# Attention and two dense layers on one core: conversions spread over the opening's turns, sinks copied between exponentials, one addition on GpSimd

## The chip, the cores and the metric

The kernel runs on one core of one Trainium2 chip. The metric is the device time of one execution in microseconds (us); of several executions the median counts. The core has TensorE (PE, matmuls and transposes into PSUM banks), VectorE (DVE), ScalarE (ACT), GpSimd (POOL) and SyncE (SP, which here issues almost all of the loads). Each engine works through its own list in order, and waits on semaphores where it needs another engine's result.

## The reference

```
scores = scale * q @ k^T                      # 2 batches, 8 heads, 768 positions, 64 wide
keep   = is_sink | in_window                  # 4 sinks, a window of 128
scores = where(keep, scores, -1e9); a = exp(scores - max)
a      = a / (sum(a) + 1e-9)
x      = (a @ v), tokens by 512
h = x @ w_in;  x = (max(h, 0) + alpha * min(h, 0)) @ w_out      # 512 -> 2048 -> 512
h = x @ w_in2; out = (h - tanh(h)) @ w_out2                     # 512 -> 2048 -> 512
```

Weights arrive as 64-bit floats and are converted on the chip to 32-bit ones.

## The kernel before

Attention is done in 48 pairs of heads. Pair n belongs to block u = n // 4 of 128 positions, and holds 2 heads. One pair goes through these helpers:

- `s_mm`: the scores by three products of split operands (L272), into two of the four banks "o".
- `s_max` (L281, VectorE): mask and row maximum, one instruction for each of the two heads. It is the first VectorE instruction of a turn.
- `s_exp` (L290, ScalarE): the exponential and its sum.
- `norm_sum`: part 0 adds 1e-9 to the two sums (L296), part 1 takes the reciprocal (L298). `norm` scales (L305), and `sink_copy` (L311) gathers the sink columns after every second pair from block 2 on.
- `t_mm` (L322) transposes the probabilities into bank t or h, `t_ev` (L329, ScalarE) copies them out. `sink_mm` (L344) transposes the sinks into a bank that scores of a later pair use too, and `sink_ev` (L348, ScalarE) copies them out.
- `pv` (L361, L362; L365 for sinks): the product with v. After four pairs `x_h` (L372, ScalarE) and `x_l` (L377, VectorE) split the block's result into a high and a low part.

Operands of the scores are split into high and low parts ahead of time: `kq_hi` (L236, ScalarE) and `kq_lo` (L239, VectorE), called by `splits_hi` and `splits_lo`. A converted weight block costs two halves on ScalarE (L73, L75) and two on VectorE (L77, L79), each over 128x1024 elements; `conv_start` issues the first two and every `conv_step` the next one. `split_w` (L217, ScalarE) and `split_lo` (L222, VectorE) split the converted weights for the products.

The order on each engine is the order in which the program is written (a manual schedule). The opening is a loop of 19 turns (S_LEAD = 19): turn n issues the scores of pair n + 1, maxima and exponentials of pair n, scaling and transposes of pair n - 1 and the product of pair n - 2, with conversions, splits and filler matmuls (`keep_busy`, L505) between. Then come 96 steps g, one for each of 2 layers, 3 chunks of 512 tokens and 16 blocks of 128 hidden columns. A step multiplies x by a block of w_in (`h_mm`, L394, 12 matmuls), copies the result out of its bank (`evac_first`, L401), applies the nonlinearity and splits it, and two steps later multiplies by w_out (`out_mm`, L446, 12 matmuls). In the first chunk all steps share bank h, so the first matmul of step g + 1 waits for the copy of step g. Pairs 19 to 47 are worked off between the products of steps 0 to 28, one in each.

## Time and profile before

| what | value |
|---|---|
| median of 3 runs (lowest, highest) | 658.94 us (657.57, 661.62) |
| the profiled execution, its span | 659.71 us, 657.9 us |
| busy of the span: PE, DVE, ACT, POOL | 97%, 80%, 72%, 0% |
| mean granted TensorE clock, share of full speed | 0.992 |

The span reaches from the first to the last instruction that the profiler saw; 1.8 us of the execution lie around it. The rows below come from timelines: start, duration, engine, line, operation, output and inputs, count, and in brackets how long the engine had been idle before and which result ended that. An instruction can start before its predecessor has drained, so the distance from one start to the next is often shorter than a duration. Windows give, for a stretch, its length, each engine's busy time with its number of instructions, the granted clock of TensorE, and the DMA engines' share and rate.

### The profile page before, as it was taken

Reading aid. Unit: us, or ns where it says so; the run is one execution under the profiler, and the core shown is the slowest. Engines: PE = TensorE matmul, PEld = TensorE weight load, DVE = VectorE, ACT = ScalarE, POOL = GpSimd, SP = SyncE. Lnnn points to the kernel's source line nnn. Section 1 sums busy time; section 2 is a strip of 40 time slices with the busy share of each in tenths; the row PEclk is TensorE's granted clock in tenths of the full one; section 3 lists DMA queues with packets and bytes.
Section 4 is the critical chain, followed back from the end, with each engine's and each line's share of the span. In section 5 each row is a group of like instructions: output and inputs, shape, how many; then the busy total and the mean of one; then the engine's idle time right before and its main releaser. Section 6 shows DMA issues by size and latency. Waiting matters only on the chain.

```text
span 657.9 us, 9271 instructions
## 1 busy us (share of the span) xinstructions
PE 638.5 (97%) x3246; PEld 503.3 (76%) x3251; DVE 528.0 (80%) x1098; ACT 471.4 (72%) x936; POOL 1.7 (0%) x9
## 2 busy tenths in 40 slices
PE   8888899999999999999999999999999999999996
PEld 3555677777777777777888888888888888888885
DVE  7976898999776665649999979888898888888884
ACT  5976888887666555556877767777777777777772
POOL 1000000000000000000000000000000000000000
PEclk9989799999999999999999999999999999999999
DMA  5643344553100000305355500000010000100001
GB/s 153 193 140 110 126 179 144 197 201 115 49 1 17 1 17 1 123 6 192 128 198 191 188 0 1 1 0 1 0 65 0 1 1 0 65 0 1 0 1 70
DMA packets 27176, 47.36 MB, mean 72 GB/s; under 512 B 3184, under 2 KB 15728, under 8 KB 27120
## 3 DMA queue, kind: packets, MB, share of 16 engines
q1 hardware_dynamic: 26400, 46.29, 20.7%
q10 hardware_dynamic: 720, 0.39, 0.3%
q8 instruction: 27, 0.44, 0.3%
q14 instruction: 29, 0.24, 0.1%
HBM read 43.53 MB, written 3.15 MB: 71 GB/s over the span
## 4 chain that ended last, share of the span: by engine, by line
PE 91%; DVE 3%; ACT 2%; DMA 2%; SPq 1%; issue 1%; DVEq 0%; ACTq 0%
PE ps_o L446 40%; PE ps_h L394 23%; PE ps_s L394 9%; PE ps_t L394 9%; PE ps_s L272 2%; PE ps_t L322 2%; PE ps_v L361 2%; PE ps_v L365 2%; PE ps_v L362 1%; DMA raw_qk<-in_qk_dram 1%; DVE pq L281 1%; SPq L181 1%; DVE pq L305 1%; DMA raw<-in_moe_w_in_dram 0%; DVE kq L239 0%
## 5 line engine op out<-in xcount | busy, mean ns | idle before, releaser
L222 DVE SCALAR_TENSOR_TENSOR wl<-wf,wh 128x512 fp32r<-128x512 f32 x192 | 123.4, 683 | 41.8 <-ACT wh L217 41.8
L217 ACT ACTIVATE wh<-wf 128x512 fp32r<-128x512 f32 x192 | 110.7, 628 | 0.1
L394 PE MATMUL ps_h<-x,wh 128*128 128x512 f32 x296 | 97.4, 409 | 3.1 <-ACT t L401 2.9
L446 PE MATMUL ps_o<-gh,wh 128*128 128x512 f32 x192 | 76.5, 398 | 0.0
L446 PE MATMUL ps_o<-gh,wl 128*128 128x512 f32 x192 | 75.0, 391 | 0.0
L446 PE MATMUL ps_o<-gl,wh 128*128 128x512 f32 x192 | 74.8, 390 | 0.0
L446 PE MATMUL ps_o<-wh,gh 128*128 128x512 f32 x192 | 74.7, 389 | 0.0
L446 PE MATMUL ps_o<-wl,gh 128*128 128x512 f32 x192 | 74.7, 389 | 0.0
L446 PE MATMUL ps_o<-wh,gl 128*128 128x512 f32 x192 | 74.7, 389 | 0.0
L394 PEld LDWEIGHTS ps_h<-x,wh 128*128 128x128 f32 x296 | 52.6, 190 | 14.6 <-ACT t L401 3.5
L290 ACT ACTIVATE pq<-pq,nm 128x288 f32<-128x288 f32 (+1 forms) x96 | 48.5, 509 | 20.5 <-DVE nm L281 20.2
L394 PE MATMUL ps_h<-x,wl 128*128 128x512 f32 x148 | 58.7, 397 | 0.2 <-DVE wl L222 0.2
L329 ACT ACTIVATE pt<-ps_t 128x512 f32<-128x512 f32 (+1 forms) x39 | 22.0, 564 | 47.3 <-PE ps_t L322 47.0
L425 ACT ACTIVATE gh<-g 128x512 fp32r<-128x512 f32 x48 | 30.4, 633 | 29.8 <-DVE g L128 29.8
L77 DVE SCALAR_TENSOR_TENSOR wf<-wf,raw 128x1024 int32<-128x1024 int32 x32 | 39.1, 1221 | 7.9 <-ACT raw L75 7.9
L446 PEld LDWEIGHTS ps_o<-gh,wh 128*128 128x128 f32 x192 | 36.1, 188 | 8.4 <-issue 1.4
L446 PEld LDWEIGHTS ps_o<-gh,wl 128*128 128x128 f32 x192 | 36.0, 188 | 7.8
L446 PEld LDWEIGHTS ps_o<-wh,gh 128*128 128x128 f32 x192 | 36.0, 188 | 7.5
L446 PEld LDWEIGHTS ps_o<-wh,gl 128*128 128x128 f32 x192 | 36.0, 188 | 7.5
L446 PEld LDWEIGHTS ps_o<-wl,gh 128*128 128x128 f32 x192 | 36.0, 188 | 7.5
L446 PEld LDWEIGHTS ps_o<-gl,wh 128*128 128x128 f32 x192 | 36.1, 188 | 7.1
L128 DVE COPY_PREDICATED g<-mask,t 128x512 f32<-128x512 int32 x48 | 36.4, 758 | 4.9
(160 smaller groups left out, 1348.9 us busy)
## 6 DMA issues: line engine op xcount, KB each, us to landing
raw<-in_moe_w_in_dram SPq DMA_DIRECT2D x32, 512.0 KB, 3.3
raw<-in_moe_w_out_dram SPq DMA_DIRECT2D x32, 512.0 KB, 4.3
raw_qk<-in_qk_dram SPq DMA_DIRECT2D x92, 64.0 KB, 3.0
vt<-in_v_dram SPq DMA_DIRECT2D x12, 256.0 KB, 2.9
out_dram<-ob SPq DMA_DIRECT2D x2, 1024.0 KB, 4.3
out_dram<-ob SPq DMA_DIRECT2D x3, 256.0 KB, 3.6
vs<-in_vsink_dram SPq DMA_DIRECT2D x2, 256.0 KB, 3.3
raw_qk<-in_qk_dram ACTq DMA_DIRECT2D x4, 64.0 KB, 2.8
```

Of the source, the lines that this page charges most:

```text
L77: nc.vector.scalar_tensor_tensor(di, di, 3, lw, op0=ALU.logical_shift_left, op1=ALU.bitwise_or)
L128: nc.vector.copy_predicated(g, mask.bitcast(I32), t)
L217: nc.scalar.activation(out=hi, in_=src, func=AF.Copy, scale=W_DOWN)
L222: nc.vector.scalar_tensor_tensor(lo, wf[m, f][:, 512 * part:512 * part + 512], W_DOWN, hi, op0=ALU.mult, op1=ALU.subtract)
L272: nc.tensor.matmul(sps[n, a][:, :w], lhsT=kq[l][h, p, at:at + 128], rhs=kq[r][h, p, K_EVEN:K_EVEN + w], start=e == 0, stop=e == 2)
L290: nc.scalar.activation(out=e, in_=e, func=AF.Exp, scale=-1.0, bias=nm[:, 2 * n + a:2 * n + a + 1], accum_out=sums[G][:, hh:hh + 1])
L322: nc.tensor.transpose(t[:, 256 * a + 128 * e:256 * a + 128 * e + 128], pq[G][:, hh + a, c:c + 128], ident)
L329: nc.scalar.activation(out=ptb[n][:, :, e0:, :], in_=tv[:, :, e0:, :], func=AF.Copy)
L361: nc.tensor.matmul(d, lhsT=vt[u - 1][:, h * D:(h + 1) * D], rhs=pt[:, a, 0, :], start=p == 0, stop=False)
L394: nc.tensor.matmul(h_ps[f], lhsT=w, rhs=x[:, r, kk, :], start=at == 0, stop=at == 11)
L425: nc.scalar.activation(out=gh, in_=mid[f], func=AF.Copy)
L446: nc.tensor.matmul(o, lhsT=l, rhs=r, start=f == 0 and e == 0, stop=f == NF - 1 and e == 2)
```

## The change

In the opening a conversion is issued one part per turn instead of two parts of ScalarE in one turn, and the conversion of block 2 begins there, in turns 16 and 17, instead of in step 0. `splits_hi` runs in the odd turns ahead of the exponentials, in the same turn as its `splits_lo`, and from step 1 on in the same step as it. `sink_ev` stands between the two exponentials instead of before both maxima. The last turn no longer issues the product of pair 16 and three fillers; step 0 starts with the 8 products that need only the high part of x, and the product of pair 16, the scores of pair 19 and the transposes of pair 17 follow. In step 0 the weights of step 1 are split before the maxima of pair 19 instead of after. The addition of 1e-9 is issued on GpSimd. `h_mm` counts single matmuls instead of threes, and `norms` is defined earlier.

```diff
             if part == 0:
-                nc.vector.tensor_scalar(r, r, 1e-9, None, op0=ALU.add)
+                nc.gpsimd.tensor_scalar(r, r, 1e-9, None, op0=ALU.add)
...
-            for G in {0: (0, 2), 1: (1,)}.get(n, (n // 2 + 2,) if n % 2 != (n < S_LEAD - 1) else ()):
+            early = n < S_LEAD
+            for G in {0: (0, 2), 1: (1,)}.get(n, (n // 2 + 1 + early,) if n > 2 and n % 2 == early else ()):
...
-                tps[n - 1] = ps_tile(["t", "h"])
+                tps[n - 1] = ps_tile("th" if n < S_LEAD - 3 else "ht"[n % 2])
                 keep_busy({0: 4, 1: 3, 2: 8}.get(n, 2), tps[n - 1])
             if n >= 2:
                 t_ev(n - 2)
-                if has_sinks(n - 2):
-                    sink_ev(n - 2)
+                if 3 <= n < S_LEAD - 2:
+                    splits_hi(n)
             s_max(n, 0)
             s_max(n, 1)
             s_exp(n, 0)
+            if n >= 2 and has_sinks(n - 2):
+                sink_ev(n - 2)
             s_exp(n, 1)
+            if n == S_LEAD - 2:
+                pv(n - 2)
             if last:
                 x_l(n - 3)
-                pv(n - 2)
-                keep_busy(3, ps_tile(["h"]))
-            if n == S_LEAD - 2:
-                pv(n - 2)
...
             for f, at in CONV0:
                 if n == at:
-                    conv_start(0, f)
-                if at < n < at + 5:
+                    conv_start(0, f, 1)
+                if at < n < at + 4:
                     conv_step(0, f)
...
             if n == S_LEAD - 3:
                 split_lo(0, 0, 0, 0)
+                conv_start(0, 2, 1)
+            if n == S_LEAD - 2:
+                conv_step(0, 2)
...
                     a_loads(n)
-                    h_mm(m, c, f, 0, 3, FIRST)
+                    h_mm(m, c, f, 0, 8, FIRST)
+                    pv(n - 3)
+                    split_w(*steps[1], 0)
+                    norms(n - 1)
+                    split_lo(*steps[1], 0)
+                    splits_lo(n - 2)
+                    s_mm(n)
                     turned(n - 2)
-                    conv_start(0, 2)
-                    h_mm(m, c, f, 3, 4, FIRST)
-                    norms(n - 1)
-                    scores(n)
+                    h_mm(m, c, f, 8, 12, FIRST)
                     conv_step(0, 2)
-                    split_w(*steps[1], 0)
-                    split_lo(*steps[1], 0)
+                    for a in range(2):
+                        s_max(n, a)
+                        s_exp(n, a)
                     evac_first(m, c, f)
                     conv_step(0, 2)
                     load_w(0, 4)
```

On ScalarE, turns 12 and 13 before: copy of transposes, two exponentials, operand split, both halves of a conversion, then turn 13's copy, sinks and exponentials.

```order
L329 ACTIVATE pt<-ps_h 128x512
L290 ACTIVATE pq,sums<-pq,nm 128x288 x2
L236 ACTIVATE kq<-raw_qk 128x2x256
L73 ACTIVATE wf,seen<-raw_90 128x1024
L75 ACTIVATE raw_90<-raw_90 128x1024
L329 ACTIVATE pt<-ps_t 128x512
L348 ACTIVATE pts<-ps_o 128x128
L290 ACTIVATE pq,sums<-pq,nm 128x288 x2
L372 ACTIVATE x<-ps_v 128x4x128
```

The same two turns now:

```order
L329 ACTIVATE pt<-ps_h 128x512
L290 ACTIVATE pq,sums<-pq,nm 128x288 x2
L73 ACTIVATE wf,seen<-raw_90 128x1024
L329 ACTIVATE pt<-ps_t 128x512
L236 ACTIVATE kq<-raw_qk 128x2x256
L290 ACTIVATE pq,sums<-pq,nm 128x288
L348 ACTIVATE pts<-ps_o 128x128
L290 ACTIVATE pq,sums<-pq,nm 128x288
L372 ACTIVATE x<-ps_v 128x4x128
L75 ACTIVATE raw_90<-raw_90 128x1024
```

One half of the conversion and the operand split moved into turn 13, and the sinks between its exponentials.

On VectorE, the maxima and the reciprocal of turn 13 before, with what each waits for:

```order
L281 ISA pq,nm<-ps_o,m_odd 128x288 [waits PE_49]
L281 ISA nm 128x1
L281 ISA pq,nm<-ps_o,m_odd 128x288 [waits Activation_49]
L281 ISA nm 128x1
L296 TENSOR_SCALAR sums<-sums 128x2
L298 RECIPROCAL sums<-sums 128x2 [waits DVE_49]
```

And now:

```order
L281 ISA pq,nm<-ps_o,m_odd 128x288 [waits PE_49]
L281 ISA nm 128x1
L281 ISA pq,nm<-ps_o,m_odd 128x288 [waits PE_49]
L281 ISA nm 128x1
L298 RECIPROCAL sums<-sums 128x2 [waits Pool_49]
```

The second maximum waited for ScalarE (the sink copy) and now waits for TensorE alone; the reciprocal waits for GpSimd.

On TensorE, from the fillers of the last turn to the first products of step 1 before (wh_701 belongs to step 0, wh_892 to step 1; rows of the same kind left out):

```order
L505 MATMUL ps_h<-idle 128x512
L394 MATMUL ps_h<-x,wh_701 128x512
...
L322 MATMUL ps_t<-ident,pq 128x128 x4
L344 MATMUL ps_o<-ident,sk 128x128
L394 MATMUL ps_h<-x,wh_701 128x512 x3
L272 MATMUL ps_o<-kq 128x288 x6
L322 MATMUL ps_t<-ident,pq 128x128 x4
L394 MATMUL ps_h<-x,wh_892 128x512 x2
```

And now (wh_699 and wh_856), from the transposes of pair 16 on:

```order
L322 MATMUL ps_t<-ident,pq 128x128 x4
L394 MATMUL ps_h<-x,wh_699 128x512
...
L361 MATMUL ps_v<-pt,vt 64x128
L362 MATMUL ps_v<-pt,vt 64x128
...
L272 MATMUL ps_o<-kq 128x288 x6
L322 MATMUL ps_t<-ident,pq 128x128 x4
L344 MATMUL ps_o<-ident,sk 128x128
L394 MATMUL ps_h<-x,wh_699 128x512 x4
L322 MATMUL ps_t<-ident,pq 128x128 x4
L394 MATMUL ps_h<-x,wh_856 128x512 x2
```

The product of pair 16 moved behind the first 8 matmuls of step 0, the scores of pair 19 ahead of its last 4, and the fillers are gone.

## Rows read from the trace of the kernel before

**Rows 1.** Windows of 20 us, the end of the opening and the first chunk

```profile
60.00:80.00 20.00, 16.86 (x88) 12.19 (x89) 13.98 (x35) 15.04 (x32) 0.00 (x0) 0.83 0.21 68
80.00:100.00 20.00, 20.00 (x114) 15.55 (x113) 19.72 (x44) 17.16 (x36) 0.00 (x0) 1.00 0.50 183
```

**Rows 2.** Timeline of VectorE, turn 10, to the first maximum of turn 11

```profile
29.99 0.45 DVE L281 CUSTOM_DVE_ANT_0 pq<-ps_o,m_even 128x288 f32<-128x288 f32 x1
...
30.74 0.16 DVE L296 TENSOR_SCALAR sums<-sums 128x2 f32<-128x2 f32 x1
30.94 0.17 DVE L298 RECIPROCAL sums<-sums 128x2 f32<-128x2 f32 x1
31.14 0.65 DVE L305 TENSOR_SCALAR pq<-pq,sums 128x288 f32<-128x288 f32 x2
...
31.97 0.68 DVE L377 TENSOR_TENSOR x<-ps_v,x 128x512 fp32r<-128x512 f32 x1
32.57 1.22 DVE L79 SCALAR_TENSOR_TENSOR wf<-raw,wf 128x1024 int32<-128x1024 int32 x1
33.70 0.45 DVE L281 CUSTOM_DVE_ANT_0 pq<-ps_o,m_even 128x288 f32<-128x288 f32 x1
```

**Rows 3.** Timeline of ScalarE, the end of turn 12 and the start of 13

```profile
37.74 0.63 ACT L236 ACTIVATE kq<-raw_qk 128x512 fp32r<-128x512 f32 x1
38.28 1.15 ACT L73 ACTIVATE wf<-raw 128x1024 f32<-128x1024 f32 x1
...
39.41 1.12 ACT L75 ACTIVATE raw<-raw 128x1024 int32<-128x1024 uint16 x1
40.43 0.57 ACT L329 ACTIVATE pt<-ps_t 128x512 f32<-128x512 f32 x1
40.91 0.26 ACT L348 ACTIVATE pts<-ps_o 128x128 f32<-128x128 f32 x1
```

**Rows 4.** Timeline of VectorE, maxima of pairs 8, 12, 13 (second), 16

```profile
23.98 0.45 DVE L281 CUSTOM_DVE_ANT_0 pq<-ps_o,m_even 128x288 f32<-128x288 f32 x1
...
36.02 0.45 DVE L281 CUSTOM_DVE_ANT_0 pq<-ps_o,m_odd 128x288 f32<-128x288 f32 x1
...
41.20 0.46 DVE L281 CUSTOM_DVE_ANT_0 pq<-ps_o,m_odd 128x288 f32<-128x288 f32 x1 [2.75 <-ACT pts L348]
...
51.41 0.45 DVE L281 CUSTOM_DVE_ANT_0 pq<-ps_o,m_even 128x288 f32<-128x288 f32 x1
```

**Rows 5.** Timeline of TensorE, a turn with sinks, then steps 1 and 2

```profile
36.52 0.71 PE L365 MATMUL ps_v<-pts,vs 128*128 128x128 f32 x4
37.16 0.67 PE L272 MATMUL ps_o<-kq 64*128 64x288 f32 x6
...
38.20 0.60 PE L322 MATMUL ps_t<-ident,pq 128*128 128x128 f32 x4
...
39.43 0.66 PE L272 MATMUL ps_o<-kq 64*128 64x288 f32 x6
...
67.75 1.22 PE L394 MATMUL ps_h<-x,wh 128*128 128x512 f32 x2 [2.89 <-ACT t L401]
...
75.78 0.73 PE L394 MATMUL ps_h<-x,wh 128*128 128x512 f32 x2
```

**Rows 6.** Timeline of GpSimd, a fill and an index pattern at the start

```profile
0.75 0.53 POOL L507 MEMSET idle<- 128x512 bf16 x1 [0.29 <-POOLq L1045]
1.30 0.24 POOL L509 IOTA rel_i<- 128x128 int32 x1
```

**Rows 7.** Timeline of ScalarE, the operand split of turn 8 and x of turn 17

```profile
26.02 0.63 ACT L236 ACTIVATE kq<-raw_qk 128x512 fp32r<-128x512 f32 x1 [0.34 <-DMA raw_qk<-in_qk_dram]
...
57.30 0.60 ACT L372 ACTIVATE x<-ps_v 128x512 fp32r<-128x512 f32 x1 [1.09 <-PE ps_v L365]
```

**Rows 8.** Timelines of VectorE and ScalarE in step 2

```profile
81.96 1.29 DVE L222 SCALAR_TENSOR_TENSOR wl<-wf,wh 128x512 fp32r<-128x512 f32 x2
...
82.40 0.62 ACT L236 ACTIVATE kq<-raw_qk 128x512 fp32r<-128x512 f32 x1
```

More of the change, by code (lines that the diff above doesn't have):

```diff
@@ L390, in h_mm @@
                 h_ps[f] = ps_tile(["hst"[turn[0] % 3]])
-            for at in range(3 * lo, 3 * hi):
+            for at in range(lo, hi):
                 kk, l, r = order[at]
@@ L564, in fast_path, with conv_start @@
         convs = {}
-        def conv_start(m, f):
+        def conv_start(m, f, k=2):
             convs[m, f] = conv_w(m, f)
-            next(convs[m, f])
-            next(convs[m, f])
+            conv_step(m, f, k)
         def conv_step(m, f, k=1):
@@ L573, in conv_step, with norms @@
                 next(convs[m, f], None)
+        def norms(n):
+            norm_sum(n, 0)
+            norm_sum(n, 1)
+            norm(n)
+            sink_copy(n)
         for n in range(S_LEAD):
@@ L590, in fast_path @@
             s_exp(n, 0)
+            if n >= 2 and has_sinks(n - 2):
+                sink_ev(n - 2)
             s_exp(n, 1)
+            if n == S_LEAD - 2:
+                pv(n - 2)
             if last:
                 x_l(n - 3)
-                pv(n - 2)
-                keep_busy(3, ps_tile(["h"]))
-            if n == S_LEAD - 2:
-                pv(n - 2)
             if n >= 1:
-                norm_sum(n - 1, 0)
-                norm_sum(n - 1, 1)
-                norm(n - 1)
-                sink_copy(n - 1)
+                norms(n - 1)
                 if not last:
@@ L608, in fast_path @@
                 pv(n - 2)
-            splits_hi(n)
+            if n < 3:
+                splits_hi(n)
             if n >= 5 and n % 4 == 1:
                 x_h(n - 2)
-            splits_lo(n)
+            if n < S_LEAD - 2:
+                splits_lo(n)
+            if last:
+                splits_hi(n - 1)
             if n >= 5 and n % 4 == 2 and not last:
@@ L622, in fast_path @@
                 if n == at:
-                    conv_start(0, f)
-                if at < n < at + 5:
+                    conv_start(0, f, 1)
+                if at < n < at + 4:
                     conv_step(0, f)
-                if n == at + 3:
+                if n == at + 3 and f + 2 < NF:
                     load_w(0, f + 2)
@@ L678, in turned @@
                 sink_ev(n)
-        def norms(n):
-            norm_sum(n, 0)
-            norm_sum(n, 1)
-            norm(n)
-            sink_copy(n)
         def scores(n):
@@ L725, in fast_path @@
                         conv_start(0, g + 2)
-                    h_mm(m, c, f, 0, 2)
+                    h_mm(m, c, f, 0, 6)
                     scores(n)
                     pv(n - 3)
-                    h_mm(m, c, f, 2, 4)
+                    h_mm(m, c, f, 6, 12)
                     evac_mid(*back)
@@ L741, in fast_path @@
                     a_loads(n)
-                    h_mm(m, c, f, 0, 3, FIRST)
+                    h_mm(m, c, f, 0, 8, FIRST)
+                    pv(n - 3)
+                    split_w(*steps[1], 0)
+                    norms(n - 1)
+                    split_lo(*steps[1], 0)
+                    splits_lo(n - 2)
+                    s_mm(n)
                     turned(n - 2)
-                    conv_start(0, 2)
-                    h_mm(m, c, f, 3, 4, FIRST)
-                    norms(n - 1)
-                    scores(n)
+                    h_mm(m, c, f, 8, 12, FIRST)
                     conv_step(0, 2)
-                    split_w(*steps[1], 0)
-                    split_lo(*steps[1], 0)
+                    for a in range(2):
+                        s_max(n, a)
+                        s_exp(n, a)
                     evac_first(m, c, f)
@@ L772, in fast_path @@
                 if mid_order:
-                    h_mm(m, c, f, 0, 4)
+                    h_mm(m, c, f, 0, 12)
                     if att_s:
@@ L814, in fast_path @@
                         load = None
-                h_mm(m, c, f, 0, 4)
+                h_mm(m, c, f, 0, 12)
                 evac_hi(*back)
@@ L833, in fast_path @@
                     break
-                h_mm(m, c, f, 0, 4)
+                h_mm(m, c, f, 0, 12)
                 if g == N - 2:
                     z = steps[g + 1]
-                    h_mm(*z, 0, 4)
+                    h_mm(*z, 0, 12)
                     out_mm(*steps[g - 2], 0, 4)
```

## The prediction

> **What bounds the kernel now.** I read the windows of 20 us first. From 80 us on TensorE is busy 20.00 of 20 us at full clock, and this row stands for the later ones, so a saving there on VectorE or ScalarE buys nothing. Before that it is not: in 60 to 80 us TensorE is busy for 16.86 us at a mean clock of 0.83, and no other engine is full either [rows 1]. So the question is only how early the saturated stretch begins, and every microsecond by which it begins earlier should come off the end. Its beginning is the hidden-layer product of step 2, at 75.78 us, the first that follows without a long wait [rows 5].
>
> Next the timelines of the opening. A turn is begun by VectorE's two row maxima (L281). The maxima of pairs 8, 12 and 16 start at 23.98, 36.02 and 51.41 us [rows 4]: turns 8 to 11 take 12.04 us and turns 12 to 15 take 15.39. The work of a turn is far less. VectorE's turn 10 is, start to start, 0.75 for the maxima, 0.20 for the addition, 0.20 for the reciprocal, 0.83 for scaling and sink copy (0.57 without the copy, estimated as the 0.65 of the row less its drain), 0.60 for a 512-column subtraction and 1.13 for half of a conversion [rows 2]. The surplus is in waits like the one of 2.75 us at 41.20 [rows 4]: in turn 12 ScalarE does both its halves of a conversion in a row (1.13 and 1.02 us), then the transposes' copy and the sink copy (40.91), and only then may VectorE take the second maximum of pair 13, which shares a bank with those sinks [rows 3]. The last row to see is TensorE's 2.89 us before step 1 at 67.75, released by ScalarE's copy of step 0 out of bank h [rows 5].
>
> **The change, part by part.** I rebuild the opening by hand with these spacings. ScalarE's are 0.48 for the transposes' copy, about 0.2 for sinks (0.26 less its drain), 0.54 for an operand split, 1.13 and 1.02 for the conversion halves [rows 3]; an exponential with its read-out takes about 0.52 (an estimate from the 0.54 of the split, the same engine and nearly the time). TensorE's are 0.64 for sink products, 1.04 for scores and fillers, 1.23 for transposes, sinks and product [rows 5].
>
> *The addition on GpSimd.* VectorE loses 0.20 us per pair. The reciprocal now waits for exponential, GpSimd and two hand-overs. The trace has no such addition; GpSimd's rows are 0.53 us for a fill of 512 columns and 0.24 for an index pattern of 128 [rows 6], against 2 columns here. With a tenth for each hand-over I take 0.4, nearer the smaller row; the ends are 0.1 and 0.73. The 0.75 us of the next pair's maxima stand between and cover it wherever VectorE, not ScalarE, is behind. In turns 1 to 7 VectorE is nearly always busy, so 7 x 0.20 = 1.4 us, less some 0.3 where operands have only just landed (the split at 26.02 had to wait 0.34 for its load [rows 7]): **1.1** (0.5 to 1.4). The maxima of pair 8 then start at 22.9.
>
> *Conversions spread, sinks between the exponentials, splits in the odd turn: turns 8 to 11.* Zero is the maxima of pair 8. ScalarE: exponentials to 1.53, first half 2.66, transposes' copy 3.14, split 3.66 (its load is there at 26.0, which is 3.1), exponentials 4.7, x 5.2, second half 6.2. VectorE: turn 8 ends at 1.52, turn 9 with the split's remainder, which waits for ScalarE, at 4.3; turn 10 does maxima, reciprocal, scaling, sinks and x to 6.7 and its conversion half to 7.8; turn 11 adds 0.75 + 0.77 + 0.60 + 1.13 to 11.1. That is **0.9** less than 12.04 (0 to 1.5).
>
> *Turns 12 to 15.* The same with sinks. ScalarE: first half to 2.66, copy 3.14, split 3.66, exponentials with the sinks between them 4.86. The second maximum no longer waits, since now the sink copy waits for it, while ScalarE would wait there for VectorE anyhow. VectorE: turn 13 ends at 4.3; turn 14 waits 0.2 for GpSimd, ends scaling at 6.3, x at 6.9, its conversion half, ready on ScalarE at 6.9, at 8.1; turn 15, with the weight split of step 0 ahead on ScalarE, ends at 11.7. **3.7** less than 15.39 (2.4 to 4.5). With all TensorE waits of this stretch now under 1 us I expect no fall of its clock here.
>
> *Turns 16 and 17.* Transposes of pair 15 can start at 1.4; then TensorE has 1.23, 1.04, a product of about 0.6 and its sinks of 0.64, and ScalarE's copy of x can start at 4.9. ScalarE's new conversion half there (1.13) ends at 2.66 and the copy for that product at 3.14, before TensorE's 3.65, so it is covered; if TensorE were faster it would cost its 1.13. Before, that copy started at 57.30 [rows 7], 5.89 after 51.41: **1.0** less (0 to 1.3). It then starts near 50.6.
>
> *First chunk's end ahead of the next pair.* Zero is the end of that copy of x, 0.5 after its start. TensorE starts step 0 at once with the 8 products that need only x's high part, where before a product and three fillers stood in front. But step 1 needs bank h back, and that copy stands on ScalarE behind the exponentials of pair 19. ScalarE: conversion half 1.02, copy 1.50, exponentials of pair 18 2.55, operand split 3.1, step 1's split 3.6. VectorE: the reciprocal of pair 18 at 2.95 (with 0.4 for GpSimd, uncovered here), scaling 3.7, weight split 4.3, operand split 4.9, conversion half 6.05, first maximum of pair 19 6.45. ScalarE again: exponentials 7.6, the copy out of h 8.1. Step 1 starts at 8.2, which is 8.7 after the copy's start, where it was 67.75 - 57.30 = 10.45: **1.8** less (0.5 to 2.8). What is late next is the same wait: TensorE has only some 5.2 us of work for these 8.2 and idles 3.0 us, as the 2.89 before, and its clock should fall again. From step 1 to step 2 I leave the 8.03 us of before [rows 5].
>
> *Later steps.* The operand split's two halves now fall in one step, so VectorE's half may wait for ScalarE's. In step 2 ScalarE's half ran from 82.40 to about 83.0 while VectorE was in its two weight splits until 83.25 [rows 8]; those cover it. Without them it is up to 0.6 us in every second step, on a VectorE that is busy 19.72 of 20 us [rows 1], though relieved of 0.20 per step. Counted at nothing; at most 0.6 in each of 8 steps of the chunk, 4.8 us. The matmul ranges in single matmuls, the moved helper and the bank names change no work.
>
> **Sum.** 1.1 + 0.9 + 3.7 + 1.0 + 1.8 = 8.5 us. The profiled execution took 659.71 us, so 651.2; the median of the three runs, 658.94, lies 0.77 under it, so **650.4**. The terms' lower ends add up to 3.4 us and the upper to 11.5; as not all fall to one side, the forecast's own range is 648 to 653.5.
>
> **Rivals.** *The clock holds.* If TensorE's idle 3.0 us should not cost the clock, step 1 runs at 2.4 GHz and step 2 hangs on ScalarE alone (copy 0.48, conversion 2.15, exponentials 1.04, a copy and two splits 1.6, the copy out of h 0.5: 5.9 for 8.03): 2.1 us more, 648.3. Against it: after the 2.89 us of before, the two matmuls at 67.75 took 1.22 us where the two at 75.78 took 0.73 [rows 5].
>
> *The engines wait for each other more than my hand schedule has it.* From turn 8 the three engines have nearly equal work, about 10 us in four turns, and each late hand-over passes on. At 0.3 us in each of 10 turns, or with the operand splits of the chunk uncovered, 3 to 4 us go: 654. For it: GpSimd's hop is in each of these loops, and VectorE's rows show how little slack step 2 has.
>
> *The addition stays uncovered: the slower end.* If GpSimd cannot work beside VectorE's maxima, the reciprocal waits for the whole of it in each of 17 turns. At 0.4 us that is 6.8 us back, 657.2; at the row of 0.53 with both hand-overs, 0.73, it is 12.4 and the end is 662.8, slower than before. It decides from 0.5 us uncovered per turn (8.5 / 17). Against it: the additions have 0.75 us of cover, and GpSimd has nothing else to do. The trace cannot say, since GpSimd's last instruction starts before any maximum. The Trainium skill, "SBUF — State Buffer", section "Who interferes with whom", speaks of this: VectorE and GpSimd share one port pair as an exclusive lock, taken by VectorE instructions with two SBUF inputs. By that rule splits and conversions would hold an addition back, but the maxima, which read one input from PSUM, would not, and the forecast stands; no row here shows it.
>
> *It doesn't do what it says.* If the 2.75 us wait hung on the conversion alone, moving the sinks adds nothing, but the conversion is spread too, so the two cannot be told apart in this sum and the time is the same.
>
> **How the numbers follow.** Forecast 0.55, clock holds 0.13, half lost 0.20, uncovered addition 0.12 (half of it slower than before by over 1%). Two in ten may be left out: the range ends at 647.5 below, to take in the clock, and at 655.5 above, to take in the half lost. A measurement of this kernel can tell about 1%, 6.6 us, from no change: 652.35 is the border. Of the forecast 0.48 lies under it and 0.07 above, the clock case all under, of the half lost 0.04: faster 0.65. Slower by over 1% is only the bad end of the addition, 0.06; the rest, 0.29, lies within.
>
> **What would show it.** In the changed kernel the maxima of pairs 8, 12 and 16 near 22.9, 34.0 and 45.7; no wait for the sink copy before a maximum; the copy of x from about 50.6, step 1 near 59.3 after about 3 us of idle with the clock at half behind it, step 2 near 67.3. I am wrong if reciprocals wait for GpSimd in most turns, if operand splits of the first chunk wait for ScalarE and step 3 and later show TensorE idle, or if a stall moves behind 80 us.

## The result and the profile after

The changed kernel takes 652.58 us (median of four runs, 652.47 to 653.42) where the kernel before takes 659.70 (median of four); the ratio is 0.9896, with a 95% interval of 0.9862 to 0.9929. That is 1.0% faster, and 2.2 us more than the 650.4 that I forecast, inside both the range and the forecast's own range. The likeliest outcome that I had named, a time under 652.35, is missed by 0.23 us; by the interval the gain is 0.7 to 1.4%, so on which side of 1% it lies is not settled. The profiled execution took 652.47 us with a span of 650.7 (before 659.71 and 657.9).

First the two windows that [rows 1] showed of before: start and end, length, busy time and instructions of PE, PEld, DVE, ACT and POOL, granted clock, DMA share, GB/s.

```profile
60.00:80.00 20.00, 18.71 (x106) 13.77 (x107) 16.83 (x39) 16.93 (x38) 2.31 (x4) 0.91 0.41 132
80.00:100.00 20.00, 20.00 (x114) 15.95 (x113) 19.05 (x42) 16.04 (x35) 2.16 (x3) 1.00 0.52 185
```

From 80 us on TensorE is full as before, and in 60 to 80 it is busy 18.71 us for 16.86. The saturated stretch begins earlier and is not itself faster.

The maxima of pairs 8, 12, 13 (both) and 16 on VectorE, which answer to [rows 4]:

```profile
23.08 0.45 DVE L281 CUSTOM_DVE_ANT_0 pq<-ps_o,m_even 128x288 f32<-128x288 f32 x1
...
34.55 0.45 DVE L281 CUSTOM_DVE_ANT_0 pq<-ps_o,m_odd 128x288 f32<-128x288 f32 x1
...
36.33 0.45 DVE L281 CUSTOM_DVE_ANT_0 pq<-ps_o,m_odd 128x288 f32<-128x288 f32 x1
...
36.84 0.46 DVE L281 CUSTOM_DVE_ANT_0 pq<-ps_o,m_odd 128x288 f32<-128x288 f32 x1
...
46.68 0.45 DVE L281 CUSTOM_DVE_ANT_0 pq<-ps_o,m_even 128x288 f32<-128x288 f32 x1
```

The second maximum of pair 13 follows the first after 0.51 us; before it waited 2.75. Turns 8 to 11 take 11.47 us (34.55 - 23.08) for 12.04, turns 12 to 15 take 12.13 for 15.39.

Behind that wait the clock fell in the kernel before, which the rows ahead do not show (clock: third number from the end):

```profile
40.00:42.00 2.00, 0.42 (x3) 0.11 (x2) 0.73 (x5) 1.98 (x6) 0.00 (x0) 1.00 0.22 65
42.00:44.00 2.00, 1.59 (x10) 1.19 (x12) 2.00 (x4) 0.33 (x2) 0.00 (x0) 0.66 0.08 23
44.00:46.00 2.00, 2.00 (x13) 1.44 (x12) 1.93 (x9) 0.38 (x1) 0.00 (x0) 0.50 0.27 54
```

In the changed kernel it is 1.00 in every window of 2 us from 4 to 60 us, as I had expected of these turns.

The copy of x and the copy out of h on ScalarE, and TensorE's last work ahead of its gap and steps 1 and 2, which answer to [rows 7] and [rows 5]:

```profile
51.92 0.60 ACT L372 ACTIVATE x<-ps_v 128x512 fp32r<-128x512 f32 x1 [0.77 <-PE ps_v L365]
...
58.98 0.53 ACT L290 ACTIVATE pq<-pq,nm 128x288 f32<-128x288 f32 x1 [1.63 <-DVE nm L281]
...
60.03 0.57 ACT L401 ACTIVATE t<-ps_h 128x512 f32<-128x512 f32 x1
```

```profile
57.36 0.60 PE L322 MATMUL ps_t<-ident,pq 128*128 128x128 f32 x4
60.66 1.22 PE L394 MATMUL ps_h<-x,wh 128*128 128x512 f32 x2 [2.70 <-ACT t L401]
...
68.15 0.73 PE L394 MATMUL ps_h<-x,wh 128*128 128x512 f32 x2 [0.61 <-ACT t L401]
```

TensorE stands idle for 2.70 us until ScalarE copies step 0 out of bank h, behind the exponentials of pair 19. The clock then falls to the lower of its two levels, as these windows of 2 us show:

```profile
58.00:60.00 2.00, 0.00 (x0) 0.00 (x0) 2.00 (x6) 1.02 (x4) 0.00 (x0) 1.00 0.00 0
60.00:62.00 2.00, 1.34 (x3) 1.15 (x4) 1.50 (x5) 2.00 (x5) 0.33 (x1) 0.63 0.25 43
62.00:64.00 2.00, 2.00 (x8) 1.16 (x9) 0.00 (x0) 1.25 (x3) 0.00 (x0) 0.52 1.02 389
64.00:66.00 2.00, 2.00 (x21) 1.58 (x18) 1.60 (x6) 1.10 (x5) 0.00 (x0) 1.00 0.68 223
```

Step 2 starts at 68.15 for 75.78, 7.63 us earlier. The last matmul starts 7.25 us earlier (644.23 for 651.48): the lead passes through the saturated stretch almost whole.

### The profile page after: what moved, and what is told of

Read it like the earlier page. It is cut to its first block, busy times and chain, and to the rows that moved or that the text cites. A ratio compares the mean times of both kernels' runs of the same rounds, so it can differ in the third digit from the quotient of the medians.

```text
span 650.7 us, 9272 instructions
## 1 busy us (share of the span) xinstructions
PE 635.4 (98%) x3243; PEld 501.9 (77%) x3248; DVE 521.0 (80%) x1050; ACT 469.7 (72%) x936; POOL 24.8 (4%) x57
## 4 chain that ended last, share of the span: by engine, by line
PE 89%; DVE 3%; DMA 2%; SPq 2%; ACT 2%; issue 1%; POOL 0%; ACTq 0%; DVEq 0%
PE ps_o L446 39%; PE ps_h L394 23%; PE ps_s L394 9%; PE ps_t L394 8%; PE ps_s L272 2%; PE ps_t L322 2%; SPq L181 2%; PE ps_v L361 2%; DMA raw<-in_moe_w_out_dram 2%; PE ps_v L365 1%; PE ps_v L362 1%; DMA raw_qk<-in_qk_dram 1%; DVE wf L77 1%; DVE pq L281 1%; ACT pq L290 0%
```

## The experiments

Of every kernel I read the same starts from the timelines and took the differences: pair 8 is the start of its first maximum, x is the copy of x, s1 and s2 are steps 1 and 2. All in us, from one profiled execution each; the medians are those of the timed runs.

| kernel | pair 8 at | turns 8-11 | turns 12-15 | 16 to x | x to s1 | s1 to s2 | s2 at | median |
|---|---|---|---|---|---|---|---|---|
| before | 23.98 | 12.04 | 15.39 | 5.89 | 10.45 | 8.03 | 75.78 | 659.70 |
| changed | 23.08 | 11.47 | 12.13 | 5.24 | 8.74 | 7.49 | 68.15 | 652.58 |
| e1_add_on_dve | 26.07 | 11.64 | 12.33 | 5.45 | 8.73 | 6.03 | 70.25 | 654.09 |
| e2_sinks_first | 22.95 | 11.75 | 13.68 | 5.25 | 8.73 | 7.44 | 69.80 | 654.19 |
| e3_conv_pairs | 23.16 | 12.38 | 12.29 | 5.89 | 8.73 | 7.04 | 69.49 | 654.42 |
| e4_sinks_only | 24.14 | 11.63 | 12.04 | 5.88 | 10.46 | 8.04 | 72.19 | 656.24 |
| e5_add_only | 22.98 | 12.23 | 14.12 | 5.88 | 10.48 | 7.02 | 72.71 | 658.33 |
| e6_product_back | 23.01 | 11.36 | 12.15 | 5.25 | 9.98 | 6.03 | 67.78 | 653.24 |
| e7_fill_gap | 23.13 | 11.37 | 12.14 | 5.24 | 8.73 | 6.01 | 66.62 | 651.15 |
| e8_copy_early | 24.60 | 11.37 | 12.13 | 5.24 | 6.26 | 7.26 | 66.86 | 650.83 |
| e9_both_copies | 23.00 | 11.36 | 12.13 | 5.24 | 6.29 | 6.18 | 64.20 | 649.78 |
| e10_add_four | 24.68 | 12.43 | 12.57 | 5.57 | 9.62 | 7.30 | 72.17 | 656.93 |
| e11_conv_only | 24.00 | 12.57 | 15.61 | 6.30 | 10.45 | 7.51 | 76.44 | 662.11 |
| e12_sinks_conv | 24.20 | 11.41 | 12.15 | 5.45 | 10.46 | 7.50 | 71.17 | 656.31 |

Where an edit does not touch a stretch, it repeats to 0.1 us or so, and pair 8 to 0.2. Some stretches also hold a fall of the clock: s1 to s2 in most kernels; the time until pair 8 in e1_add_on_dve and e8_copy_early; turns 12 to 15 in the kernel before and in e5_add_only; and in e11_conv_only all three from turn 8 to the copy of x.

**The sinks and the conversions, in the kernel before.** First the sink copy alone.

```diff
             if n >= 2:
                 t_ev(n - 2)
-                if has_sinks(n - 2):
-                    sink_ev(n - 2)
             s_max(n, 0)
             s_max(n, 1)
             s_exp(n, 0)
+            if n >= 2 and has_sinks(n - 2):
+                sink_ev(n - 2)
             s_exp(n, 1)
```

> The kernel before with the sink copy moved between the exponentials and nothing else. Theory (the waits of VectorE for the sink copy, 4.4 us in three, vanish, but ScalarE is still late with two halves in a row, and its exponentials are waited for instead): 2 to 3 us earlier at step 2 and at the end than the kernel before. Rival (the two conversion halves in a row alone set the time): 0 to 0.5 us earlier.

Measured: 656.24 us, ratio 0.9951 (0.9930 to 0.9972). Step 2 comes 3.59 us earlier, more than I expected, and turns 12 to 15 alone give 3.35 of it: 12.04 for 15.39, as short as in the changed kernel. In these turns the two halves in a row cost nothing once no maximum waits for the sink copy. The clock may have a part in the 3.35: in the kernel before it fell behind the first wait, and here it stays at 1.00. But VectorE waits for nothing in those turns except the sink copy, 2.75 us and then 1.00 at 49.46, so the clock can account for the second wait at most, 1.00 us. Of the lead 0.9 us is lost later (2.68 are left at the last matmul), in part here (ScalarE, then TensorE):

```profile
154.90 1.15 ACT L73 ACTIVATE wf<-raw 128x1024 f32<-128x1024 f32 x1 [1.75 <-DMA raw<-in_moe_w_out_dram]
```

```profile
160.29 0.74 PE L394 MATMUL ps_h<-x,wh 128*128 128x512 f32 x2 [0.50 <-ACT t L401]
```

ScalarE waits for the raw weights of a coming conversion, its copy out of h is late by that, and TensorE idles 0.50 us. The kernel before has no wait at this place.

Then the spread of the conversions alone. VectorE's two halves, which follow those of ScalarE, come one turn later by it.

```diff
-        def conv_start(m, f):
+        def conv_start(m, f, k=2):
...
-                    conv_start(0, f)
+                    conv_start(0, f, 1)
```

> The kernel before with ScalarE's conversion halves of turns 8 and 12 spread over two turns and nothing else (the sinks stay ahead of both maxima). With the sinks alone moved, turns 12 to 15 went from 15.39 to 12.04 us. Theory (either part alone takes away most of the long wait, so that their gains do not add up): turns 12 to 15 near 13.7, turns 8 to 11 near 11.5, step 2 and the end about 2 us earlier than the kernel before. Rival (the conversion does nothing without the sinks' move): within 0.5 us of the kernel before.

Measured: 662.11 us, ratio 1.0034 (1.0017 to 1.0051): 0.3% slower. Theory and rival both miss. The longest wait for the sink copy is shorter, but there are four now, 5.6 us in all for 4.4 in three, and a new one has come in turn 11:

```profile
33.48 0.46 DVE L281 CUSTOM_DVE_ANT_0 pq<-ps_o,m_even 128x288 f32<-128x288 f32 x1 [1.08 <-ACT pts L348]
...
41.02 0.46 DVE L281 CUSTOM_DVE_ANT_0 pq<-ps_o,m_odd 128x288 f32<-128x288 f32 x1 [1.84 <-ACT pts L348]
```

And the clock falls twice in the opening, where it fell once before (42 to 46 us). The first time is in 34 to 38, though TensorE is busy for 1.31 us of 34 to 36, and in the kernel before for 0.90 with the clock at 1.00:

```profile
34.00:36.00 2.00, 1.31 (x6) 0.98 (x8) 1.93 (x6) 0.71 (x3) 0.00 (x0) 0.68 0.16 54
36.00:38.00 2.00, 2.00 (x14) 1.45 (x12) 1.93 (x8) 1.44 (x4) 0.00 (x0) 0.50 0.24 47
```

The second is in 50 to 56 us (0.94, 0.50, 0.70), where the kernel before has 1.00. How much of the loss is the clock's and how much the waits', no run separates.

Last, both of them together, the two diffs above in one kernel.

> The kernel before with both the sink copy between the exponentials and ScalarE's conversion halves spread over two turns, and nothing else; the operand splits stay in the even turns and the addition on VectorE. The sinks alone gave a copy of x at 53.69 us, the spread alone made it later, 58.48 against 57.30. Theory (the spread loses only where a maximum waits for the sink copy; without that wait it pays as it does in the changed kernel): turns 8 to 11 near 11.2, turns 12 to 15 near 12.0, the copy of x 0.5 to 1.8 us earlier than with the sinks alone, near 52.5, end 1 us earlier than there, about 655. Rival (the spread pays only with the operand splits in the odd turns): the copy of x at 53.7 or later, and the end no earlier than with the sinks alone, 656.2 or more.

Measured: 656.31 us, ratio 0.9954 (0.9935 to 0.9973). The copy of x comes at 53.21, 0.48 us earlier than with the sinks alone, just under the 0.5 to 1.8 of the theory; the median is no earlier, as the rival had it (the last matmul of the profiled execution is, by 0.58), with 0.53 us of TensorE's time lost at 159.59 after another wait for raw weights (1.80 us on ScalarE at 154.22). So with the sinks moved, the spread turns from a loss of 1.2 us at the copy of x, the falls of the clock included, into a gain of 0.5, and the gain is not seen in the median here.

**The same two, taken out of the changed kernel.** The sinks back ahead of both maxima:

```diff
                 t_ev(n - 2)
+                if has_sinks(n - 2):
+                    sink_ev(n - 2)
...
             s_exp(n, 0)
-            if n >= 2 and has_sinks(n - 2):
-                sink_ev(n - 2)
             s_exp(n, 1)
```

> The changed kernel with the sink copy before both maxima again, as in the kernel before. Theory (the long wait of the kernel before came from the sink copy standing behind two conversion halves; with one half it is short): the second maxima of turns 13, 15 and 17 wait 0.5 to 1.1 us each, and step 2 and the end are 1 to 1.5 us later, about 653.9. Rival (where the sinks stand is most of the gain of turns 12 to 15): 3 us later or more, 655.6.

Measured: 654.19 us, ratio 0.9938 (0.9911 to 0.9964). Turns 12 to 15 take 1.55 us more, step 2 is 1.65 later; the wait is back in turns 13 and 15 (and 0.63 in turn 17), near what the theory said and far from the rival's 3:

```profile
38.15 0.46 DVE L281 CUSTOM_DVE_ANT_0 pq<-ps_o,m_odd 128x288 f32<-128x288 f32 x1 [1.21 <-ACT pts L348]
...
45.50 0.46 DVE L281 CUSTOM_DVE_ANT_0 pq<-ps_o,m_odd 128x288 f32<-128x288 f32 x1 [1.06 <-ACT pts L348]
```

ScalarE's two halves back in one turn, and VectorE's one turn earlier with them:

```diff
-                    conv_start(0, f, 1)
+                    conv_start(0, f)
```

> The changed kernel with ScalarE's two conversion halves of turns 8 and 12 in one turn again, the sinks still between the exponentials. Theory (both parts count): ScalarE is a half, about 1.1 us, late at the start of turns 9 and 13, VectorE's maxima of pairs 12 and 16 and step 2 start 1 to 2 us later, end about 654. Rival (the sinks' place did it alone): within 0.5 us of the changed kernel.

Measured: 654.42 us, ratio 0.9930 (0.9903 to 0.9958). Turns 8 to 11 take 0.91 us more, the turns from 16 to the copy of x 0.65 more, turns 12 to 15 only 0.16: 1.7 us in all, as the theory had it. At step 2 it is 1.34, since this execution spent 0.45 us less in step 1. Here then the spread is worth more than in e12_sinks_conv (1.7 for 0.5); the kernels also differ in the place of the operand splits and of the addition, and which of them makes this difference I did not separate; no run moves the operand splits by themselves.

**The addition.** Back on VectorE in the changed kernel:

```diff
-                nc.gpsimd.tensor_scalar(r, r, 1e-9, None, op0=ALU.add)
+                nc.vector.tensor_scalar(r, r, 1e-9, None, op0=ALU.add)
```

> The changed kernel with the addition of 1e-9 back on VectorE. Theory (VectorE sets the pace of the opening, and GpSimd takes 0.20 us per pair off it): the maxima of pair 8 start near 24.0 instead of 23.08, step 2 near 70 instead of 68.15, and the end is 1.5 to 3 us later than the changed kernel, about 654.5. Rival (the wait for GpSimd's addition costs as much as it saves): positions and end within 0.5 us of the changed kernel.

Measured: 654.09 us, ratio 0.9923 (0.9893 to 0.9952). The positions mislead until the clock is taken out of them. The eight fillers of turn 2 take 3.39 us in this kernel (first fence) and 1.90 in the changed one (second), so that the operand split of turn 3 waits 1.79 us:

```profile
11.85 3.39 PE L505 MATMUL ps_t<-idle 128*128 128x512 bf16 x8
```

```profile
10.58 1.90 PE L505 MATMUL ps_t<-idle 128*128 128x512 bf16 x8
```

In 8 to 10 us TensorE was busy 0.35 of 2.00 us here and 1.45 in the changed kernel, and the granted clock in 12 to 14 is 0.50 for 1.00. The edit alone does not decide this: e8_copy_early, which differs from the changed kernel only from step 0 on, has the slow fillers too, and e12_sinks_conv, with the addition on VectorE as here, has not. What the edit does is seen behind it: turns 4 to 7 take 9.03 us (26.07 - 17.04) for 8.21, so the addition costs its 0.20 us in each; turns 8 to 11 and 12 to 15 take 0.17 and 0.20 more in all four turns together; from pair 4 to the copy of x it is 1.40. In step 1, on the other hand, this execution kept the full clock, and won 1.46 us by that. The rival (no difference) falls; the theory holds for turns 4 to 7. The end, 1.51 us later, has the clock's part in both places in it and is not the price of the addition alone.

The addition alone moved, in the kernel before (the same line the other way round):

> The kernel before with the addition of 1e-9 on GpSimd and nothing else. Theory (0.20 us per pair leave VectorE, covered by the next maxima): the maxima of pair 8 start near 23.1 instead of 23.98, and the end is 1 to 2 us earlier than the kernel before. Rival (the reciprocal waits for GpSimd): no gain, or later by up to 3 us.

Measured: 658.33 us, ratio 0.9976 (0.9958 to 0.9993). Pair 8 starts at 22.98, 1.00 us earlier, as the theory said. Turns 12 to 15 are 1.27 us shorter as well; the second wait for the sink copy, 1.00 in the kernel before, is 0.38 there. The profiled execution is 3.07 us ahead at step 2, 1.01 of it by a shorter step 1, while the median of ten runs is only 1.25 us under the 659.58 of the kernel before beside them. That goes with the clock: the three runs with a mean granted clock of 0.994 or more, the profiled one among them, took 656.54 to 656.99 us, the seven at 0.991 or 0.992 took 658.08 to 659.91.

Four additions of a quarter each in place of one:

```diff
-                nc.gpsimd.tensor_scalar(r, r, 1e-9, None, op0=ALU.add)
+                for _ in range(4):
+                    nc.gpsimd.tensor_scalar(r, r, 2.5e-10, None, op0=ALU.add)
```

> The changed kernel with GpSimd's addition done in four quarters, one behind the other, on the same two columns: some 0.6 us more on GpSimd for each pair, of no use to the result. Theory (the 0.75 us of the next pair's maxima cover the addition, where VectorE is what is behind): one addition has 0.3 us or more to spare, so a part of the 0.6 shows, 0.1 to 0.3 us per turn: step 2 and the end 2 to 5 us later than the changed kernel. Rival (the addition is on the path already, so that every 0.2 us of it counts): 0.6 us in each of 17 turns, 10 us later, 662. The other rival (GpSimd is of no account whatever it takes): within 0.5 us.

Measured: 656.93 us, ratio 0.9960 (0.9946 to 0.9974), 4.35 us above the changed kernel; step 2 is 4.02 later, which is 0.24 us in each of 17 turns for the 0.63 that were added. The waits of the opening (us in total, times, longest; lines stand one lower here) are now

```profile
DVE sums L299 <- POOL sums L297: 6.3, 12, 2.0
```

where the changed kernel has

```profile
DVE sums L298 <- POOL sums L296: 1.1, 1, 1.1
```

So, on the average of the turns, one addition is covered with some 0.4 us to spare (an estimate, 0.63 - 0.24); four are not.

**The end of the opening and step 1.** The product of pair 16 and three fillers back in front of step 0:

```diff
             if last:
                 x_l(n - 3)
+                pv(n - 2)
+                keep_busy(3, ps_tile(["h"]))
...
                     h_mm(m, c, f, 0, 8, FIRST)
-                    pv(n - 3)
```

> The changed kernel with the product of pair 16 and three fillers in front of step 0 again. Theory (step 1 hangs on ScalarE's copy out of h, which hangs on the exponentials of pair 19, not on TensorE, which idles 2.70 us there): step 1 within 0.4 us of 60.66, the idle time before it 1 us shorter, the end within 0.5 us of the changed kernel. Rival (TensorE's earlier start on step 0 was the gain): step 1 and the end 1 to 2 us later.

Measured: 653.24 us, ratio 0.9900 (0.9867 to 0.9933). The theory falls and the rival holds for step 1, which is 9.98 us behind the copy of x for 8.74. VectorE's and TensorE's rows:

```profile
59.57 0.46 DVE L281 CUSTOM_DVE_ANT_0 pq<-ps_o,m_even 128x288 f32<-128x288 f32 x1 [1.17 <-ACT pts L348]
```

```profile
61.75 0.73 PE L394 MATMUL ps_h<-x,wh 128*128 128x512 f32 x2 [1.59 <-ACT t L401]
```

TensorE does the transposes and sinks of pair 17 later, so ScalarE's sink copy is later, and the maximum of pair 19 waits for that, and behind it the exponentials and the copy out of h. TensorE's early start is on the path, through the sinks. But after 1.59 us of idle the clock stays up, step 1 takes 6.03 us instead of 7.49, and step 2 starts at 67.78, 0.22 us earlier than in the changed kernel when counted from the copy of x. What the early start wins, the clock takes. The median is 0.66 us over that of the changed kernel, but the runs (652.29 to 654.42) lie on both sides of its four, and a wait of TensorE of 0.81 us at 156.49, behind a late load, is in the profiled one; so the end decides nothing here.

Twelve fillers behind the transposes of pair 18:

```diff
                 turned(n - 1)
+                if g == 0:
+                    keep_busy(12, ps_tile(["o"]))
```

> The changed kernel with twelve filler matmuls, of no use to the result, behind the transposes of pair 18 in step 0, so that TensorE is busy for most of the 2.70 us ahead of step 1. Theory (the idle time is followed by half clock, which costs time in step 1): the granted clock stays at 1.00 from 58 to 66, step 1 starts within 0.3 us of 60.66, step 2 follows about 6.0 to 6.5 us later instead of 7.49, the end about 1 us earlier, 651.5. Rival (step 2 hangs on ScalarE and VectorE at either clock): step 2 and the end within 0.3 us.

Measured: 651.15 us, ratio 0.9872 (0.9843 to 0.9902); the theory holds. Steps 1 and 2:

```profile
60.61 0.73 PE L394 MATMUL ps_h<-x,wh 128*128 128x512 f32 x2
...
66.62 0.73 PE L394 MATMUL ps_h<-x,wh 128*128 128x512 f32 x2 [0.61 <-ACT t L401]
```

The clock is 1.00 in every window from 56 to 72 us, step 1 starts where it did, and step 2 follows after 6.01 us: the lower clock costs 1.48.

The copy out of h ahead of the maxima and exponentials of pair 19:

```diff
                     h_mm(m, c, f, 8, 12, FIRST)
+                    evac_first(m, c, f)
+                    turned(n - 1)
                     conv_step(0, 2)
                     for a in range(2):
                         s_max(n, a)
                         s_exp(n, a)
-                    evac_first(m, c, f)
...
                 splits_hi(n)
-                turned(n - 1)
+                if g:
+                    turned(n - 1)
```

> The changed kernel with ScalarE's copy of step 0 out of bank h, and the transposes of pair 18 on TensorE, ahead of the maxima and exponentials of pair 19 instead of behind them. Theory (step 1 hangs on that copy, which hangs on the exponentials of pair 19): step 1 starts near 58 instead of 60.66 and step 2 near 65.5 instead of 68.15, the end near 650. Rival (the exponentials of pair 19 come late in turn and are waited for in step 1, before step 2): step 1 earlier, step 2 and the end at most 1 us earlier.

Measured: 650.83 us, ratio 0.9859 (0.9826 to 0.9891). Counted from the copy of x, step 1 is 2.48 us earlier and step 2 2.71 (13.52 for 16.23), as the theory said; that copy itself is 1.42 late, by the clock in turns 2 and 3. The clock stays at 1.00 in step 1 here, and e7_fill_gap wins 1.49 of the 2.71 by that alone (14.74 from the copy of x to step 2), so 1.22 are left for the earlier copy. The next late thing is the same copy, one step on:

```profile
59.60 0.73 PE L394 MATMUL ps_h<-x,wh 128*128 128x512 f32 x2 [0.25 <-ACT t L401]
...
66.86 0.73 PE L394 MATMUL ps_h<-x,wh 128*128 128x512 f32 x2 [1.84 <-ACT t L401]
```

So the last one moves that too, on top of e8_copy_early:

```diff
                     evac_mid(*back)
                     if g + 2 < NF:
                         conv_step(0, g + 2)
+                    if g == 1:
+                        evac_first(m, c, f)
+                        split_w(*steps[2], 0)
+                        split_lo(*steps[2], 0)
                     evac_hi(*back)
```

(with the three calls left out further down for that step).

> The kernel of e8_copy_early with the same done in step 1: ScalarE's copy of step 1 out of bank h and the weight split of step 2 stand ahead of the splits of step 0's result, on VectorE the weight split's remainder ahead of the result's. In e8_copy_early TensorE then idled 1.84 us ahead of step 2, released by that copy, which started at 66.22 though TensorE had ended step 1 at 64.5. Theory (that copy is again what is late next): it starts 1.5 us earlier, step 2 starts 5.9 to 6.5 us after step 1 instead of 7.26, and the end is about 0.9 us earlier than there for equal starts, 649.9. Rival (the weights of later steps are then waited for from the DMA, near 150 us, and the gain is given back there): step 2 earlier, but the idle time before the step near 155 longer by as much, end as e8_copy_early, 650.8.

Measured: 649.78 us, ratio 0.9851 (0.9827 to 0.9875), the fastest of all; its five runs (649.36 to 650.74) lie wholly under the four of the changed kernel, and overlap the four of e8_copy_early (649.38 to 652.10). Step 2 follows step 1 after 6.18 us, now behind ScalarE's weight split:

```profile
64.20 0.73 PE L394 MATMUL ps_h<-x,wh 128*128 128x512 f32 x2 [0.76 <-ACT wh L217]
```

It starts 3.95 us earlier than in the changed kernel; the last matmul 3.09 earlier (641.14). There is no wait for weights near 155 in this execution, so the rival did not come about here.

## Why the prediction was right, point by point

**What bounds the kernel.** Right. Every term that I took from the opening arrives at the end: 7.63 us at step 2, 7.25 at the last matmul.

**The addition on GpSimd**, 1.1 us until pair 8: 0.90 between the two profiles, 1.00 in e5_add_only. Turns 4 to 7 give 0.20 each, as forecast; turns 0 to 3 only 0.09 and 0.19 in all (pair 4 at 14.87 and 14.77 for 14.96). I had left out that it is worth little after turn 8 in the changed kernel, 0.2 us in four turns (e1_add_on_dve); in the kernel before it gave 1.27 in turns 12 to 15 (e5_add_only), where it shortened a wait that the sinks' move takes away anyhow.

**Turns 8 to 11**, 0.9: 0.57. **Turns 12 to 15**, 3.7: 3.26. **Turns 16 and 17**, 1.0: 0.65. The mechanism is right and the sizes are 0.33 to 0.44 too large. Two waits have grown in the opening, in us, times and longest:

```profile
ACT pq L290 <- DVE nm L281: 5.1, 6, 1.6
...
DVE kq L239 <- ACT kq L236: 2.8, 4, 1.2
```

Before they were 1.9 and 1.1 us. The misses in turns 8 to 15 can be placed at VectorE's waits for ScalarE:

```profile
27.19 0.69 DVE L239 TENSOR_TENSOR kq<-raw_qk,kq 128x512 fp32r<-128x512 f32 x1 [0.99 <-ACT kq L236]
...
38.38 0.69 DVE L239 TENSOR_TENSOR kq<-raw_qk,kq 128x512 fp32r<-128x512 f32 x1 [0.31 <-ACT kq L236]
...
41.90 1.23 DVE L77 SCALAR_TENSOR_TENSOR wf<-wf,raw 128x1024 int32<-128x1024 int32 x1 [0.33 <-ACT raw L75]
```

Behind the first, turn 9 ends 4.72 us after the maxima of pair 8 (27.80 - 23.08) where my schedule had 4.3, and turns 10 and 11 add nothing to that. Behind the other two, turn 13 ends 4.43 us after the maxima of pair 12 (forecast 4.3) and turn 14 after 8.50 (forecast 8.1). My hand schedule had ScalarE ready earlier than it was; this much of the rival of engines that wait for each other came true. In turns 12 to 15 the cause was put too broadly: I named ScalarE's two halves in a row and the sink copy behind them as one thing. e4_sinks_only and e11_conv_only take them apart: the sinks' place alone gives 3.35 us there, the spread alone loses 0.22. The fall of the clock that went away can be at most 1.00 us of the 3.35. The rival that the sinks' move adds nothing falls by the first of these. The spread earns its part elsewhere, in turns 8 to 11 and 16 and 17 (e3_conv_pairs).

**First chunk's end ahead of the next pair**, 1.8: 1.71, with step 1 8.74 us behind the copy of x (forecast 8.7), 2.70 us of idle (3.0) and the clock down behind it, as said. The steps between come out too: counted from 0.5 us behind the start of the copy of x, the reciprocal of pair 18 starts at 2.96 (forecast 2.95) and the exponentials of pair 19 end at 7.61 (7.6). The chain named, through the exponentials of pair 19 to the copy out of h, is shown by e8_copy_early. TensorE's earlier start is worth 1.24 of the 1.71 (9.98 - 8.74 in e6_product_back); the other 0.47, with the weight split and the conversion of block 2 moved, no run takes apart.

**Step 1 to step 2**, left at 8.03: 7.49, a gain of 0.54 that I had not counted, since the clock was up again at 64 us. For the sum this was luck: e11_conv_only and e12_sinks_conv have 7.51 and 7.50 too, the kernel before and e4_sinks_only 8.03 and 8.04, and what decides it is not shown. **The clock holds**, a rival at 2.1 us more: e7_fill_gap measures 1.48, with step 2 6.01 us behind step 1 (forecast 5.9, though its parts add up to 5.8). The against (2.89 us of idle before) was right for the profiled execution; in e1_add_on_dve the clock did hold behind the same idle time.

**Later steps**, at nothing: 0.37 us given back, 0.26 in step 2, where TensorE waits for the remainder of a weight split, and 0.11 at 301.56, where it waits 0.34 for one instead of 0.23. The operand splits of the chunk are not waited for, and the timeline shows no wait of TensorE between 80 and 300 us.

**The uncovered addition.** It did not come about: the reciprocal waits for GpSimd for more than 0.2 us once, at 55.38, and there most of the time is ScalarE's exponential, which ends only just before the addition:

```profile
54.85 0.20 ACT L290 ACTIVATION_READ_ACCUMULATOR pq<-pq,nm 128x1 f32 x1
```

```profile
55.38 0.17 DVE L298 RECIPROCAL sums<-sums 128x2 f32<-128x2 f32 x1 [1.13 <-POOL sums L296]
```

From the end of that exponential, 55.05, to the reciprocal it is 0.33 us, the addition and both hand-overs together, for the 0.4 that I had taken. In e10_add_four, with 0.63 us more, it costs 0.24 per turn; the price of the mechanism was real, the slack was there.

The sum of 8.5 is 1.2 us too large: the five terms by 1.4 together, less the 0.54 of step 1 to step 2, plus the 0.37 given back. The other 0.9 us of the 2.2 are not in the kernel: 0.8 because the median of the kernel before is 659.70 here and was 658.94 when I took it, 0.1 between profiles and medians.

## What to carry to other kernels

Find the first moment from which an engine is full, and cost a change only by how much earlier that moment comes; what is won there came out at the end nearly whole, until loads were late. When an instruction waits behind a queue of work on another engine, move the waited-for instruction first and spread the work second: here the move alone gave all that turns 12 to 15 had to give, and the spread alone made the kernel slower. Look for the same copy again one step on after each such move (60.66, then 66.86), and cost the clock together with an idle stretch: useless matmuls in it moved the step behind it by nothing and the next one by 1.5 us (e7_fill_gap).

## What the hardware showed that I had not expected

**GpSimd's addition is stretched by VectorE's instructions with two inputs in SBUF.** Three additions of the changed kernel, the last of which is the usual 0.21 us:

```profile
33.53 1.18 POOL L296 TENSOR_SCALAR sums<-sums 128x2 f32<-128x2 f32 x1 [1.98 <-ACT pq L290]
...
46.18 0.66 POOL L296 TENSOR_SCALAR sums<-sums 128x2 f32<-128x2 f32 x1 [2.50 <-ACT pq L290]
...
55.14 0.21 POOL L296 TENSOR_SCALAR sums<-sums 128x2 f32<-128x2 f32 x1 [3.69 <-ACT pq L290]
```

What VectorE did beside the first two:

```profile
33.42 1.22 DVE L79 SCALAR_TENSOR_TENSOR wf<-raw,wf 128x1024 int32<-128x1024 int32 x1
...
45.54 1.22 DVE L79 SCALAR_TENSOR_TENSOR wf<-raw,wf 128x1024 int32<-128x1024 int32 x1
```

Both additions end within 0.1 us of the conversion half that was running when they began (34.71 and 34.64, 46.84 and 46.76). Beside the maxima, which read one input from PSUM, an addition takes its 0.21 us (at 23.48, for one), and so does one that starts 0.05 us ahead of a weight split with two inputs in SBUF (at 48.40). The Trainium skill, "SBUF — State Buffer", section "Who interferes with whom", says this: VectorE and GpSimd share a port pair, and a VectorE instruction with two SBUF inputs contends with a GpSimd instruction that reads SBUF. The prediction cited it as a rule that no row bore out; these rows agree with it. In the changed kernel it costs nothing, since the maxima come between.

**The clock does not fall after every idle stretch of the same length.** After 2.70 to 2.72 us without work ahead of step 1, step 1 took 7.49 us in the changed kernel and 7.44 in e2_sinks_first at the lower level, 7.04 in e3_conv_pairs, where the clock fell only from 64 us on, and 6.03 in e1_add_on_dve, where it stayed at 1.00. The same in turns 2 and 3: e12_sinks_conv kept 1.00 after 0.47 us of work in 8 to 10 us, e8_copy_early fell to 0.50 after 0.90. These are different kernels, but executions of one kernel differ in the same way: of the four of e1_add_on_dve two had a mean clock of 0.998 and took 653.18 and 653.41 us, two had 0.995 and took 654.77 and 654.92. That is up to 1.5 us in one place and more than a microsecond in the other, as much as most edits here are worth, and why I compare stretches and not only ends.

**Loads can be what is late next.** Five of the kernels (e4, e6, e8, e11, e12) have a wait of TensorE of 0.28 to 0.81 us near 155 to 165 us, each behind ScalarE's wait of 1.5 to 2.1 us for a load; the changed kernel's ScalarE waits 0.68 at 150.04 without harm, and the kernel before and the others have none at this place or one that is covered. It does not follow how early the kernel is there, and I did not find out what sets it.
